# Decode block on one core: cache tiles loaded as K0 V0 K1 V1 K2 K3 V2 V3, the output weights as one load, and up's first sums ahead of gate's turn

## The chip, the core and the metric

The kernel runs on one core of one Trainium2 chip. A core has five engines that each work through their own queue: TensorE (PE in the profile, with its weight loads as PEld), VectorE (DVE), ScalarE (ACT), GpSimd (POOL) and SyncE (SP), which here only issues DMAs. The DMAs run on 16 DMA engines. The metric is the device time of one execution in microseconds (us).

## What is computed

One token goes through a pre-norm transformer block: attention over a cache of 4096 positions with 32 heads of 128, and a gated feed-forward of width 1728. All tensors are bf16, the model width is 640.

```python
def block(x, k_cache, v_cache, wq, wo, w_gate, w_up, w_down):
    q = (layernorm(x) @ wq)                  # 32 heads of 128
    scores = q . k_cache * 128 ** -0.5       # 32 x 4096
    p = softmax(scores)
    o = p @ v_cache                          # 32 x 128
    h = x + o.reshape(4096) @ wo             # 640
    g, u = layernorm(h) @ w_gate, layernorm(h) @ w_up    # 1728
    return h + (gelu(g) * u) @ w_down        # 640
```

Each weight and each cache entry is used once. K and V caches are 33.6 MB each, wq and wo 5.2 MB each, the three feed-forward weights 2.2 MB each.

## The kernel before

**Tiles and slots.** The heads are taken in four groups G of eight. A tile is the K or the V of one group: 128 partitions (16 for each head) by 256 positions by 128, which is 64 KB in each partition. Three slots of that size in on-chip memory hold everything large: slot 2 first holds wq, slots 0 and 1 the first K and V; then the tiles follow each other through the slots in load order (`home`). At the end wo lies in slot 2 and the feed-forward weights in slot 0; slot 1 takes small rows of the tail.

**Order of work.** The program is written out by hand. `Prog` (line 39) keeps one list of operations for each engine with their dependences; `emit` turns these into semaphore waits. What stands in an engine's list runs in that order. All large loads are issued by SyncE (`dma`, line 60), in the order in which they stand in the program: an issue whose wait isn't over holds back all that follow it. A load waits until the tile that it overwrites has been read (`done`).

The load order before is wq, K0, V0, K1, V1, K2, V2, K3 (in two halves), V3, wo (two halves of 16 heads' rows), then w_down's last rows, w_gate, w_up in two parts, and the rest of w_down in six. K1 waits for the use of wq, V1 for K0, K2 for V0, V2 for K1, K3 for V1, V3 for K2, wo for V2 and the feed-forward weights for K3.

**Scores.** For each group there are eight chunks c of 32 positions. `score_mult` (L315) multiplies K by q in place on VectorE, 128 x 4096 elements; its `fold` (L323 and, through the helper `matmul_again`, L29) sums the products on TensorE by eight matmuls against the identity into one of two PSUM banks, c % 2; `score_sum` (L332) reduces that bank on VectorE. VectorE's list is multiply c, then the sum of c - 1, so that it works while TensorE folds.

**Softmax and values.** `softmax` (L337 to L346) makes the exponentials on ScalarE and spreads them on VectorE into `mix`, the left operand of `attend` (L358): 64 matmuls of 128 x 512 against V. The source calls a group of 16 of them `pv`. In the kernel before `attend(G)` stands right behind `softmax(G)` on TensorE, and so ahead of the folds of group G + 1. `pick(G)` (L364 to L368) takes each head's part out of the result on VectorE; it stands behind the first sum of the next group. `head_sum(G)` (L372, L374) adds up the partitions of each head on TensorE, at c = 3.

**Output projection.** Two groups of heads share a result of 16 rows. `normalize(t)` (L378, L379) divides by the softmax sums, `spread(t)` (L382) and `take(t)` (L386, L391) turn it into columns `aP`, and `proj_part(t)` (L403 and L29) multiplies these by half t of wo in 32 matmuls. The first half runs for t = 0 within group 2's chunks 4 to 6 and behind the last `attend`; t = 1 follows at the end.

**Feed-forward.** The projection's rows are turned into columns (L462 to L470), added to x, normalized (L276 to L282, L479). `glu` (L490) makes gate and up in 20 matmuls each; `turn` (L496, L500, L503) copies such a row and turns it into columns, by VectorE for gate and by ScalarE for up. `resid` (L510) puts h into the output's bank. TensorE's list is gate, `resid`, gate's turn, up's first 12 matmuls, its last 8, and up's turn. VectorE and ScalarE make the gelu (L518 to L525), `down` (L540) multiplies by w_down in 57 matmuls in the order of the parts' loads, and the row is copied (L557, L559) and written out.

Of the kernel before, what the change touches and what calls it, by code (L numbers as in the profile page):

```python
# [5 lines left out]
FP32 = mybir.dt.float32  # L6
BF16 = mybir.dt.bfloat16
# [103 lines left out]
def bass_sequential_preLN__gqa_block_cached__glu_gated_geglu__decode_kernel(nc, A_x, A_k_cache, A_v_cache, A_wq, A_wo, B_x, B_w_gate, B_w_up, B_w_down, out):  # L111
# [17 lines left out]
    rz = sb("rz", [16, 2], FP32)  # L129
    po_r = sb("po_r", [128, 2, DH + 1], FP32)  # L130
    m4 = sb("m4", [128, 4], FP32)
    hs = sb("hs", [128, 24], FP32)
    hb = sb("hb", [128, 24], FP32)
    hbx = sb("hbx", [128, 8, 4], BF16)
    aT = sb("aT", [16, 2, 128], BF16)
    aP = sb("aP", [128, 2, 16], BF16)
    sel = sb("sel", [16, 16, 8], BF16)
    m8 = sb("m8", [128, 8], FP32)
    aM = sb("aM", [128, 8, 16], FP32)
# [34 lines left out]
    m8_t = first_t.take(128).rearrange("p (a b) -> p a b", a=8)  # L174
# [21 lines left out]
    wo_sb = slots[2][:, 0:32 * D].rearrange("p (t i n) -> p t i n", t=2, i=16)  # L196
# [18 lines left out]
    def load(kind, G, half, *deps):  # L215
        src = A_k_cache if kind == "K" else A_v_cache
        src = src[0, 8 * G:8 * G + 8, :, :].rearrange("h (p r) d -> (h p) (r d)", p=16)
        lo, hi = (0, SLOT) if half is None else (SLOT // 2 * half, SLOT // 2 * half + SLOT // 2)
        landed[(kind, G, half)] = P.dma("sync", home[(kind, G)][:, lo:hi], src[:, lo:hi], *deps)
# [5 lines left out]
    load("K", 0, None)  # L225
    load("V", 0, None)
# [18 lines left out]
    c_hb = mask(hb[:, 8:16], ones_b[:, 0:8], [[-16, 8]], 0, 1, ALU.is_ge, c_bz)  # L245
    c_hb = mask(hb[:, 8:16], hb[:, 8:16], [[16, 8]], 15, -1, ALU.is_ge, c_hb)
# [7 lines left out]
    c_sel = mask(sel[:, :, :], ones_b[0:16, 0:128].rearrange("p (a b) -> p a b", a=16), [[1, 16], [0, 8]], 0, -1, ALU.is_equal)  # L254
    c_m8 = mask(m8_t, ones_b[:, 0:128].rearrange("p (a b) -> p a b", a=8), [[-1, 8], [-8, 16]], 0, 1, ALU.is_equal)
# [3 lines left out]
    c_odd = V(lambda e: e.reduce_sum(odd[:, :], hb[:, 8:16].rearrange("p (a b) -> p b a", b=2), axis=AX.X), c_hb)  # L259
    c_far = V(lambda e: e.tensor_scalar(far[:, :, :], odd[:, :].unsqueeze(2).to_broadcast([128, 2, 16]), -1e38, 1e38, ALU.mult, ALU.add), c_odd)  # L260
    c_m4 = V(lambda e: e.reduce_sum(m4[:, :], m4_t, axis=AX.X), c_m4)
    c_m8 = V(lambda e: e.reduce_sum(m8[:, :], m8_t, axis=AX.X), c_m8)
    c_hs = V(lambda e: e.reduce_sum(hs[:, 8:16], hs_t.rearrange("p a b c -> p a (b c)"), axis=AX.X), c_hs, c_hz)
# [38 lines left out]
    free2 = [qd, c_sel2, c_par, c_m4, c_m8, c_hs, c_idb]  # L302

    folds, reds, exps, pbs, pvs, mks, evs, hds, nbs = {}, {}, {}, {}, {}, {}, {}, {}, {}
    z4s, spr, aPs = {}, {}, {}
# [6 lines left out]
    def score_mult(G, c):  # L312
        kt = tile("K", G)[:, 32 * c:32 * c + 32, :]
        got = landed.get(("K", G, None)) or landed[("K", G, c // 4)]
        m = V(lambda e: e.tensor_tensor(out=kt, in0=kt, in1=qb[:, G, :].unsqueeze(1).to_broadcast([128, 32, DH]), op=ALU.mult),  # L315
              got, q1)
        again, held[0] = held[0], True

        def fold(e):
            for b in range(8):  # L320
                args = (ps_f[c % 2][:, :], id_b[:, :], kt[:, :, 16 * b:16 * b + 16])
                if b == 0 and not again:
                    i = e.matmul(*args, start=True, stop=False)  # L323
                else:
                    i = matmul_again(nc, *args, b == 0, b == 7, (128, 128), (0, 0))
            return i
        folds[(G, c)] = T(fold, m, c_idb, reds.get((G, c - 2) if c >= 2 else (G - 1, c + 6)))
        if c == 7:
            done[("K", G)] = folds[(G, c)]
# [22 lines left out]
    def attend(G):  # L352
        vt = tile("V", G)
        for n in range(PARTS):
            def pv(e, n=n):
                for c in range(64 // PARTS * n, 64 // PARTS * (n + 1)):
                    a = 32 * (c % 4)
                    i = e.matmul(po[a:a + 32, 0:512], p_bd[:, c, :], vt[:, 4 * c:4 * c + 4, :],  # L358
                                 start=(c < 4), stop=(c >= 60))
                return i  # L360
            pvs[G] = done[("V", G)] = other(pv, pbs[(G, n)], landed[("V", G, None)], mks.get(G - 1))
# [15 lines left out]
    def normalize(t):  # L377
        rc = V(lambda e: e.reciprocal(rz[:, t:t + 1], ps_a[0:16, 132 * t + DH:132 * t + DH + 1]), hds[2 * t + 1])  # L378
        z4s[t] = V(lambda e: e.tensor_scalar(aT[:, t, :], ps_a[0:16, 132 * t:132 * t + DH], rz[:, t:t + 1], None, ALU.mult), rc)  # L379

    def spread(t):
        spr[t] = other(lambda e: e.matmul(ps_z[:, 32:160], sel[:, :, :].rearrange("p a b -> p (a b)"), aT[:, t, :], start=True, stop=True),  # L382
                       z4s[t], c_sel)

    def take(t):
        m = V(lambda e: e.tensor_tensor(out=aM[:, :, :], in0=ps_z[:, 32:160].rearrange("p (q i) -> p q i", q=8),  # L386
                                        in1=m8[:, :].unsqueeze(2).to_broadcast([128, 8, 16]), op=ALU.mult), spr[t], c_m8)

        def fn(e):
            with nc.allow_low_precision(reason="one of the eight terms is not zero"):  # L390
                return e.reduce_sum(aP[:, t, :], aM[:, :, :].rearrange("p q i -> p i q"), axis=AX.X)  # L391
        aPs[t] = V(fn, m)

    def proj_part(t, lo, hi, *ws):
        def fn(e):
            for i4 in range(lo, hi, 4):
                for half in range(2):
                    for i in range(i4, i4 + 4):
                        a = 32 * (i - i4)
                        args = (bank[half][a:a + 1, 0:320], aP[:, t, i:i + 1], wo_sb[:, t, i, 320 * half:320 * half + 320])  # L400
                        start, stop = t == 0 and i < 4, t == 1 and i >= 12
                        if half == 0:
                            r = e.matmul(*args, start=start, stop=stop)  # L403
                        else:
                            r = matmul_again(nc, *args, start, stop, (128, 32), (0, a))
            return r
        return T(fn, *ws)

    PARTS = 4
    for G in range(NG):  # L410
        for c in range(8):
            score_mult(G, c)
            if c >= 1:
                score_sum(G, c - 1)
            if c == 1 and G:
                pick(G - 1)
            if c == 3 and G:
                head_sum(G - 1)
            if c == 4 and G == 2:
                normalize(0)  # L420
            if c == 5 and G == 2:
                spread(0)
            if c == 6 and G == 2:
                take(0)
        score_sum(G, 7)
        softmax(G)
        if G == 0:
            load("K", 1, None, *free2)
            load("V", 1, None, done[("K", 0)])
        attend(G)  # L430
        if G == 0:
            load("K", 2, None, done[("V", 0)])
        if G == 1:
            load("V", 2, None, done[("K", 1)])
            for h in range(2):
                load("K", 3, h, done[("V", 1)])
        if G == 2:
            load("V", 3, None, done[("K", 2)])
# [153 lines left out]
```

## Time and profile before

| | |
|---|---|
| time, median of 3 runs | 202.01 us (201.98 to 202.13) |
| the profiled execution's own time | 202.1 us |
| its span, first to last instruction | 200.9 us |
| bytes read | 84.23 MB, 419 GB/s over the span |
| busy: PE, PEld, DVE, ACT, POOL | 110.0, 17.7, 118.5, 6.8, 4.2 us |
| mean granted TensorE clock | 0.832 |

The profile shows one execution. Its page gives each engine's busy time, the span in 40 slices (a digit is the busy share in tenths, PEclk the granted clock), the DMA queues, the chain of work that ended last, the costliest groups of instructions and the DMA issues with the time from issue to landing. The trace behind it answers by timeline: start, duration, engine, line, operation, tiles and, in brackets, how long the engine had been idle and what released it. By stretches it gives each engine's busy time, then three figures: granted clock, mean share of the DMA engines in use, GB/s. SPq stands for SyncE's queue, where the issues are.

The chain that ended last is 51% DMA, 30% DVE and 16% PE. The longest group is the multiply of L315, 32 times 2282 ns.

### The profile page before, as it was taken

Reading aid. Unit: us, or ns where it says so; the run is one execution under the profiler, and the core shown is the slowest. Engines: PE = TensorE matmul, PEld = TensorE weight load, DVE = VectorE, ACT = ScalarE, POOL = GpSimd, SP = SyncE. Lnnn points to the kernel's source line nnn. Section 1 sums busy time; section 2 is a strip of 40 time slices with the busy share of each in tenths; the row PEclk is TensorE's granted clock in tenths of the full one; section 3 lists DMA queues with packets and bytes.
Section 4 is the critical chain, followed back from the end, with each engine's and each line's share of the span. In section 5 each row is a group of like instructions: output and inputs, shape, how many; then the busy total and the mean of one; then the engine's idle time right before and its main releaser. Section 6 shows DMA issues by size and latency. Waiting matters only on the chain.

```text
span 200.9 us, 1518 instructions
## 1 busy us (share of the span) xinstructions
PE 110.0 (55%) x771; PEld 17.7 (9%) x491; DVE 118.5 (59%) x160; ACT 6.8 (3%) x18; POOL 4.2 (2%) x19
## 2 busy tenths in 40 slices
PE   0108000686665708776745196856394777394584
PEld 0103000000002200000011000000120000131322
DVE  3300100889975027999750569897869997624331
ACT  2100000000001000000010000000100000100111
POOL 7100000000000000000000000000000000000000
PEclk9999855599996665899979757999789999888567
DMA  9999999999999999999999999799999998999993
GB/s 359 416 478 418 418 418 418 418 431 483 522 431 418 396 431 431 418 431 418 418 418 434 444 522 431 339 418 424 431 502 421 431 431 372 445 404 441 404 408 108
DMA packets 3178, 84.32 MB, mean 420 GB/s; under 512 B 354, under 2 KB 868, under 8 KB 1380
## 3 DMA queue, kind: packets, MB, share of 16 engines
q1 hardware_dynamic: 3170, 84.23, 97.8%
q8 instruction: 5, 0.08, 0.2%
q14 instruction: 1, 0.01, 0.0%
q10 hardware_dynamic: 2, 0.00, 0.0%
HBM read 84.23 MB, written 0.00 MB: 419 GB/s over the span
## 4 chain that ended last, share of the span: by engine, by line
DMA 51%; DVE 30%; PE 16%; SPq 1%; issue 1%; ACT 0%
DMA slot<-in_A_k_cache_dram 39%; DVE slot L315 21%; DMA slot<-in_B_w_down_dram 12%; PE bank L29 8%; DVE sc L332 6%; PE bank L358 6%; SPq L60 1%; PE bank L323 1%; DVE mix L364 1%; PE bank L540 1%; DVE mix L346 0%; DVE mix L367 0%; DVE mx L337 0%; ACT p_t L342 0%; DVE po_r L368 0%
## 5 line engine op out<-in xcount | busy, mean ns | idle before, releaser
L315 DVE TENSOR_TENSOR slot<-slot,qb 128x4096 bf16<-128x4096 bf16 x32 | 72.7, 2282 | 32.7 <-DMA slot<-in_A_k_cache_dram 32.7
L29 PE MATMUL bank<-slot,id_b 128*128 128x512 bf16 x248 | 66.2, 419 | 21.7 <-DVE slot L315 21.7
L332 DVE TENSOR_REDUCE sc<-bank 128x32 f32<-128x512 f32 x32 | 21.9, 685 | 12.4 <-PE bank L29 12.4
L358 PE MATMUL bank<-slot,mix 128*32 128x512 bf16 x256 | 22.1, 521 | 12.3 <-DVE mix L346 12.3
L323 PE MATMUL bank<-slot,id_b 128*128 128x512 bf16 x8 | 3.8, 471 | 33.5 <-DVE slot L315 33.5
L358 PEld LDWEIGHTS bank<-slot,mix 128*32 128x32 bf16 x256 | 8.3, 126 | 72.1 <-DVE mix L346 61.3
L297 PE MATMUL bank<-slot,xlnM 128*32 128x512 bf16 x40 | 4.5, 630 | 7.3 <-DMA slot<-in_A_wq_dram 7.3
L342 ACT ACTIVATE p_t<-sc,nb 128x256 bf16<-128x256 f32 x4 | 2.0, 507 | 161.8 <-DVE nb L341 161.8
L346 DVE TENSOR_TENSOR mix<-p_t,hbx 128x512 bf16<-128x512 bf16 x16 | 5.7, 420 | 2.7 <-ACT p_t L342 2.7
L301 DVE CAST qb<-bank 128x512 bf16<-128x512 f32 x1 | 0.7, 692 | 10.3 <-PE bank L297 10.3
L490 PE MATMUL bank<-slot,hlnT 128*1 128x512 bf16 (+1 forms) x40 | 4.6, 551 | 1.5 <-DVE hlnT L479 1.5
L364 DVE TENSOR_TENSOR mix<-bank,m 128x512 f32<-128x512 f32 x4 | 2.7, 684 | 4.4 <-PE bank L358 4.4
L270 PE MATMUL bank<-one_bf,slot 1*128 1x1 bf16 x5 | 0.4, 177 | 6.8 <-DMA slot<-in_A_x_dram 6.8
L323 PEld LDWEIGHTS bank<-slot,id_b 128*128 128x128 bf16 x8 | 0.8, 98 | 36.8 <-DVE slot L315 36.3
L372 PEld LDWEIGHTS bank<-po_r,hb 128*16 128x16 f32 x8 | 0.5, 94 | 36.6 <-issue 36.5
L403 PE MATMUL bank<-slot,aP 128*1 128x320 bf16 x32 | 2.2, 299 | 1.0 <-DMA slot<-in_A_wo_dram 1.0
L540 PE MATMUL bank<-slot,hm 128*1 128x128 bf16 (+2 forms) x57 | 2.2, 255 | 0.7 <-DMA slot<-in_B_w_down_dram 0.7
L297 PEld LDWEIGHTS bank<-slot,xlnM 128*32 128x32 bf16 x40 | 1.6, 140 | 9.4 <-issue 9.4
L29 PE MATMUL bank<-slot,aP 128*1 128x320 bf16 x32 | 2.2, 299 | 0.0
L557 DVE CAST slot<-bank 1x128 bf16<-1x128 f32 (+1 forms) x2 | 0.6, 316 | 2.4 <-PE bank L540 2.4
L374 PE MATMUL bank<-po_r,hs 128*16 128x128 f32 x8 | 1.5, 272 | 0.5 <-DVE po_r L368 0.5
L367 DVE TENSOR_TENSOR mix<-mix 128x256 f32<-128x256 f32 x4 | 1.7, 424 | 0.1
(91 smaller groups left out, 40.7 us busy)
## 6 DMA issues: line engine op xcount, KB each, us to landing
slot<-in_A_k_cache_dram SPq DMA_DIRECT2D x2, 4096.0 KB, 38.0
slot<-in_A_wq_dram SPq DMA_DIRECT2D x1, 5120.0 KB, 15.4
slot<-in_A_wo_dram SPq DMA_DIRECT2D x2, 2560.0 KB, 30.9
slot<-in_B_w_gate_dram SPq DMA_DIRECT2D x1, 2160.0 KB, 17.1
slot<-in_B_w_up_dram SPq DMA_DIRECT2D x1, 1296.0 KB, 19.7
slot<-in_B_w_down_dram SPq DMA_DIRECT2D x2, 640.0 KB, 23.0
slot<-in_B_w_up_dram SPq DMA_DIRECT2D x1, 864.0 KB, 21.4
slot<-in_B_w_down_dram SPq DMA_DIRECT2D x1, 480.0 KB, 24.3
```

The lines of the kernel that those rows point to most:

```text
L29: return e.add_instruction(mybir.InstMatmult(name=nc.get_next_instruction_name(), engine=e.engine, start_tensor_calc=start, stop_tensor_ca ...
L60: ev = self.op(eng, lambda e: e.dma_start(out, in_), *deps, dma=True)
L297: i = e.matmul(ps_q[32 * j:32 * j + 32, :], xlnM[:, 160 * s + 32 * c:160 * s + 32 * c + 32], wq_j[:, c, 2 * j + s, :, :], start=(c == 0 an ...
L315: m = V(lambda e: e.tensor_tensor(out=kt, in0=kt, in1=qb[:, G, :].unsqueeze(1).to_broadcast([128, 32, DH]), op=ALU.mult), got, q1)
L323: i = e.matmul(*args, start=True, stop=False)
L332: reds[(G, c)] = V(lambda e: e.reduce_sum(sc[:, 32 * c:32 * c + 32], ps_f[c % 2][:, :].rearrange("p (g d) -> p g d", d=16), axis=AX.X), fo ...
L346: pbs[(G, n)] = pbs[G] = V(lambda e, lo=lo, hi=hi: e.tensor_tensor(out=p_bd[:, lo:hi, :].rearrange("p c (a r) -> p c a r", a=8), in0=p_t[: ...
L358: i = e.matmul(po[a:a + 32, 0:512], p_bd[:, c, :], vt[:, 4 * c:4 * c + 4, :], start=(c < 4), stop=(c >= 60))
L364: mks[G] = V(lambda e: e.tensor_tensor(out=po_m, in0=po[:, 0:512].rearrange("p (b d) -> p b d", b=4), in1=m4[:, :].unsqueeze(2).to_broadca ...
L403: r = e.matmul(*args, start=start, stop=stop)
L490: i = e.matmul(po[32 * a:32 * a + 1, 512 * k:512 * k + n], hlnT[:, c:c + 1], w[:, c, 512 * a:512 * a + n], start=(c == 0), stop=(c == 4))
L540: i = e.matmul(ps_d[32 * q:32 * q + 1, a - lo:b - lo], w, wd_sb[:, m, a - base:b - base], start=False, stop=(m == 12), skip_group_check=(m ...
```

## The change

Six things are edited.

- The load order becomes K0 V0 K1 V1 K2 K3 V2 V3, every tile in one load. K3 now waits for K1, V2 for V1, V3 for K2. K3 lies in slot 2 and V2 in slot 0.
- wo becomes one load. It waits for K3, whose slot it takes; the feed-forward weights, which stand behind it in SyncE's list, wait for V2.
- `attend(2)` moves from behind `softmax(2)` to chunk 5 of group 3, between the folds of chunks 4 and 5. `pick(2)` moves to chunk 7 of group 3 and `head_sum(2)` behind `softmax(3)`.
- The four groups share one result of 32 rows. `head_sum` puts each group's sums into it by masks of 32 columns. `normalize` runs once, at the end, with the spreading and taking in it.
- `proj` runs once, 64 matmuls behind the landing of all of wo.
- TensorE's list in the tail becomes gate, up's first 12 matmuls, gate's turn, up's last 8, `resid`, up's turn.

Masks grow or go with it: `hs` and `hb` have 56 columns instead of 24, `sel` is 32 x 32 x 4, and the mask `m8` is no longer made.

```diff
-    order = [(kind, G) for G in range(NG) for kind in "KV"]
+    order = [("K", 0), ("V", 0), ("K", 1), ("V", 1), ("K", 2), ("K", 3), ("V", 2), ("V", 3)]
     for n, t in enumerate(order):
         home[t] = slots[n % 3][:, :]
-    home[("K", 3)], home[("V", 2)] = slots[0][:, :], slots[2][:, :]
...
     def head_sum(G):
-        g, at = G % 2, 132 * (G // 2)
-        other(lambda e: e.matmul(ps_a[0:16, at + DH:at + DH + 1], hb[:, 8 - 8 * g:24 - 8 * g], po_r[:, g, DH:DH + 1],
-                                 start=(g == 0), stop=(g == 1), skip_group_check=True), exps[G], z4s.get(G // 2 - 1), c_hb)
-        hds[G] = T(lambda e: e.matmul(ps_a[0:16, at:at + DH], hs[:, 8 - 8 * g:24 - 8 * g], po_r[:, g, 0:DH],
-                                      start=False, stop=(g == 1), skip_group_check=True), evs[G], c_hs)
+        lo = 24 - 8 * G
+        other(lambda e: e.matmul(ps_a[0:32, DH:DH + 1], hb[:, lo:lo + 32], po_r[:, G % 2, DH:DH + 1],
+                                 start=(G == 0), stop=(G == 3), skip_group_check=True), exps[G], c_hb)
+        hds[G] = T(lambda e: e.matmul(ps_a[0:32, 0:DH], hs[:, lo:lo + 32], po_r[:, G % 2, 0:DH],
+                                      start=False, stop=(G == 3), skip_group_check=True), evs[G], c_hs)
...
         for c in range(8):
+            if c == 5 and G == 3:
+                attend(2)
             score_mult(G, c)
             if c >= 1:
                 score_sum(G, c - 1)
-            if c == 1 and G:
+            if c == 1 and G in (1, 2):
                 pick(G - 1)
-            if c == 3 and G:
+            if c == 3 and G in (1, 2):
                 head_sum(G - 1)
-            if c == 4 and G == 2:
-                normalize(0)
-            if c == 5 and G == 2:
-                spread(0)
-            if c == 6 and G == 2:
-                take(0)
+            if c == 7 and G == 3:
+                pick(2)
         score_sum(G, 7)
         softmax(G)
...
-        attend(G)
+        if G == 3:
+            head_sum(2)
+        if G != 2:
+            attend(G)
...
         if G == 1:
-            load("V", 2, None, done[("K", 1)])
-            for h in range(2):
-                load("K", 3, h, done[("V", 1)])
+            load("K", 3, done[("K", 1)])
+            load("V", 2, done[("V", 1)])
...
-    d_wo = [P.dma("sync", wo_sb[:, t, :, :], A_wo[2048 * t:2048 * t + 2048, :].rearrange("(p i) n -> p i n", i=16), done[("V", 2)])
-            for t in range(2)]
-    free = done[("K", 3)]
+    d_wo = P.dma("sync", slots[2][:, 0:32 * D], A_wo[:, :].rearrange("(p i) n -> p (i n)", i=32), done[("K", 3)])
+    free = done[("V", 2)]
...
     pick(NG - 1)
-    proj_part(0, 0, 16, aPs[0], d_wo[0], reds[(NG - 1, 7)])
     head_sum(NG - 1)
-    normalize(1)
-    spread(1)
-    take(1)
-    pr = proj_part(1, 0, 16, aPs[1], d_wo[1])
+    aPd = normalize()
+    pr = T(proj, aPd, d_wo, reds[(NG - 1, 7)])
...
     ga = T(glu(0, wg_sb, range(5)), hl, d_wg, mks[NG - 1])
+    T(glu(1, wu_sb, range(3)), d_wu[0], c_po)
+    ga = turn(0, ps_g, ga, z0)
+    up = T(glu(1, wu_sb, range(3, 5)), d_wu[1])
     T(resid, hx, c_onef)
-    ga = turn(0, ps_g, ga, z0)
-    T(glu(1, wu_sb, range(3)), d_wu[0], c_po)
-    up = T(glu(1, wu_sb, range(3, 5)), d_wu[1])
```

More of the change, by code (lines that the diff above doesn't have):

```diff
@@ L207, in bass_sequential_preLN__gqa_block_cached__glu_gated_geglu__decode_kernel, with load @@
     home = {}
-    order = [(kind, G) for G in range(NG) for kind in "KV"]
+    order = [("K", 0), ("V", 0), ("K", 1), ("V", 1), ("K", 2), ("K", 3), ("V", 2), ("V", 3)]
     for n, t in enumerate(order):
         home[t] = slots[n % 3][:, :]
-    home[("K", 3)], home[("V", 2)] = slots[0][:, :], slots[2][:, :]
     tile = lambda kind, G: home[(kind, G)].rearrange("p (k d) -> p k d", d=DH)
     landed, done = {}, {}
-    def load(kind, G, half, *deps):
+    def load(kind, G, *deps):
         src = A_k_cache if kind == "K" else A_v_cache
         src = src[0, 8 * G:8 * G + 8, :, :].rearrange("h (p r) d -> (h p) (r d)", p=16)
-        lo, hi = (0, SLOT) if half is None else (SLOT // 2 * half, SLOT // 2 * half + SLOT // 2)
-        landed[(kind, G, half)] = P.dma("sync", home[(kind, G)][:, lo:hi], src[:, lo:hi], *deps)
+        landed[(kind, G)] = P.dma("sync", home[(kind, G)], src, *deps)
     A(lambda e: e.preload_act_table_set("natural_log_exp_and_others"))
@@ L224, in bass_sequential_preLN__gqa_block_cached__glu_gated_geglu__decode_kernel @@
     d_wq = P.dma("sync", wq_sb, A_wq[:, :].rearrange("(p c) n -> p (c n)", c=5))
-    load("K", 0, None)
-    load("V", 0, None)
+    load("K", 0)
+    load("V", 0)
     c_one = V(lambda e: e.memset(one_bf[:, :], 1.0))
@@ L313, in score_mult @@
         kt = tile("K", G)[:, 32 * c:32 * c + 32, :]
-        got = landed.get(("K", G, None)) or landed[("K", G, c // 4)]
         m = V(lambda e: e.tensor_tensor(out=kt, in0=kt, in1=qb[:, G, :].unsqueeze(1).to_broadcast([128, 32, DH]), op=ALU.mult),
-              got, q1)
+              landed[("K", G)], q1)
         again, held[0] = held[0], True
@@ L360, in pv @@
                 return i
-            pvs[G] = done[("V", G)] = other(pv, pbs[(G, n)], landed[("V", G, None)], mks.get(G - 1))
+            pvs[G] = done[("V", G)] = other(pv, pbs[(G, n)], landed[("V", G)], mks.get(G - 1))
     def pick(G):
@@ L377, in normalize @@
[L377 to L387, printed above, removed]
-        def fn(e):
-            with nc.allow_low_precision(reason="one of the eight terms is not zero"):
-                return e.reduce_sum(aP[:, t, :], aM[:, :, :].rearrange("p q i -> p i q"), axis=AX.X)
-        aPs[t] = V(fn, m)
@@ L394, in proj_part @@
[L394 to L407, printed above, removed]
+        lo = 24 - 8 * G
@@ new lines, in head_sum, with normalize @@
+        other(lambda e: e.matmul(ps_a[0:32, DH:DH + 1], hb[:, lo:lo + 32], po_r[:, G % 2, DH:DH + 1],
+                                 start=(G == 0), stop=(G == 3), skip_group_check=True), exps[G], c_hb)
+        hds[G] = T(lambda e: e.matmul(ps_a[0:32, 0:DH], hs[:, lo:lo + 32], po_r[:, G % 2, 0:DH],
+                                      start=False, stop=(G == 3), skip_group_check=True), evs[G], c_hs)
+    def normalize():
+        rc = V(lambda e: e.reciprocal(rz[:, :], ps_a[0:32, DH:DH + 1]), hds[3])
+        z = V(lambda e: e.tensor_scalar(aT[:, :], ps_a[0:32, 0:DH], rz[:, 0:1], None, ALU.mult), rc)
+        sp = T(lambda e: e.matmul(ps_z[:, 32:160], sel[:, :, :].rearrange("p a b -> p (a b)"), aT[:, :], start=True, stop=True), z, c_sel)
+        m = V(lambda e: e.tensor_tensor(out=aM[:, :, :], in0=ps_z[:, 32:160].rearrange("p (q i) -> p q i", q=4),
+                                        in1=m4[:, :].unsqueeze(2).to_broadcast([128, 4, 32]), op=ALU.mult), sp, c_m4)
+        def fn(e):
+            with nc.allow_low_precision(reason="one of the four terms is not zero"):
+                return e.reduce_sum(aP[:, :], aM[:, :, :].rearrange("p q i -> p i q"), axis=AX.X)
+        return V(fn, m)
@@ new lines, in proj @@
+    def proj(e):
+        for i4 in range(0, 32, 4):
+            for half in range(2):
+                for i in range(i4, i4 + 4):
+                    a = 32 * (i - i4)
+                    args = (bank[half][a:a + 1, 0:320], aP[:, i:i + 1], wo_sb[:, i, 320 * half:320 * half + 320])
+                    if half == 0:
+                        r = e.matmul(*args, start=(i < 4), stop=(i >= 28))
+                    else:
+                        r = matmul_again(nc, *args, i < 4, i >= 28, (128, 32), (0, a))
+        return r
```

41 lines of the change are left out of this document (18 added, 23 removed).

## The prediction

> **What bounds the kernel now.** I read the page's slices and DMA queues first, then the chain that ended last, then the timeline of the attention loop and the tail.
>
> ```profile
> DMA  9999999999999999999999999799999998999993
> q1 hardware_dynamic: 3170, 84.23, 97.8%
> slot<-in_A_wq_dram SPq DMA_DIRECT2D x1, 5120.0 KB, 15.4
> ```
>
> The 16 DMA engines are busy in all slices but the last: one stream of 84 MB in issue order, each load waiting its turn. Any time in which they have nothing issued is added to the end, and so is the tail behind the last landing. The last load (96 KB of w_down, issued 180.12, landing 18.7 us later by the DMA issues) is there at 198.8; the span ends at 200.9. So I ask of each moved load: is it issued before the one ahead of it runs out? These are SyncE's issues and the rows that the change moves against them:
>
> ```profile
> 34.76 4.50 DVE L315 TENSOR_TENSOR slot<-slot,qb 128x4096 bf16<-128x4096 bf16 x2 [14.03 <-DMA slot<-in_A_k_cache_dram]
> ...
> 59.60 0.33 SPq L60 DMA_DIRECT2D slot<-in_A_v_cache_dram  x1
> ...
> 140.58 0.33 SPq L60 DMA_DIRECT2D slot<-in_A_v_cache_dram  x1
> ...
> 144.51 4.49 DVE L315 TENSOR_TENSOR slot<-slot,qb 128x4096 bf16<-128x4096 bf16 x2
> ...
> 148.94 0.80 SPq L60 DMA_DIRECT2D slot<-in_A_wo_dram  x2
> ...
> 169.09 1.89 PE L29 MATMUL bank<-slot,id_b 128*128 128x512 bf16 x8 [0.91 <-DVE slot L315]
> 171.00 0.33 SPq L60 DMA_DIRECT2D slot<-in_B_w_down_dram  x1
> ...
> 183.26 0.31 PE L403 MATMUL bank<-slot,aP 128*1 128x320 bf16 x4 [1.05 <-DMA slot<-in_A_wo_dram]
> ...
> 188.94 1.87 PE L490 MATMUL bank<-slot,hlnT 128*1 128x512 bf16 x17 [1.49 <-DVE hlnT L479]
> ...
> 198.07 1.17 PE L540 MATMUL bank<-slot,hm 128*1 128x128 bf16 x20 [0.67 <-DMA slot<-in_B_w_down_dram]
> ```
>
> V3 is issued at 140.58 and lands on the last engine 30.3 us later, at 170.9; the trace's completion counts show the first engine done at 169.0. Behind it stands wo, issued at 148.94, 20 us early. The other weights wait for K3's last fold and go out at 171.00, covered by wo's 12 us on the engines. The profiled execution took 202.1 us, 1.2 over its span and 0.1 over the median of 202.01. The sum is made against it.
>
> **The change part by part.**
>
> *wo behind K3's last fold (the costly step).* wo's slot now holds K3, not V2, so wo waits for that fold, and the ten weight loads stand behind it on SyncE's queue although their own wait (PV of V2) is long over. When is the fold? K2 still lands fourth after wq, at 112.5. VectorE leaves K2's loop earlier by the first normalization: 129.69 to 130.14 (L378, L379) and 135.74 to 136.33 (L386, L391), 1.05 us. The first K3 multiply, at 144.51 before, comes at 143.5. K3's loop then has no PV ahead of its first fold and no pick at c=1, which makes it K0's loop: 34.76 to the issue released by its last fold at 59.60, 24.84 us, with a first fold at half clock (PE has been idle for 6 us in both). That gives 168.3.
>
> Now PV of V2 sits between folds 4 and 5. Its 64 matmuls took 5.25 us in group 2, 31 of them at half clock; the 33 after 146.95 took 1.9, so all at full clock take 3.7. Fold 5 then ends 1.93 + 3.7 + 1.9 = 7.55 us after multiply 4, where VectorE, with two sums (0.60) and two multiplies (2.20), has been ready since 5.6. The stall is 1.95 us. The pick at c=7 (1.4) lies beside fold 7. wo is issued at **170.3**, when the first engines have been dry for 1.3 us and the last is about to be.
>
> *Restart.* No run here shows a restart in mid-kernel, but the launch is one: wq, of wo's size and row length, was issued at 0.0; 15 engines finished it by 14.6 and the last at 15.4, where the packets alone (8 of 1.514 us on each engine) take 12.1. Nearest from below is the output, 1.1 us from issue to landing, which would give 13.2. I take 14.6, the same load from idle engines: wo lands at 184.9 (183.5 to 185.7), not at 183.1. The page "DMA: Bandwidth & Descriptors" of the Trainium skill (Specifications) puts the first byte of a SyncE load at about 0.6 us, where wq's first packet starts at 1.0; by the page the landing would be an estimated 184.5 and the time 204.2. Its rule to issue early and wait late (Rules for kernel authors) speaks against this edit, by the 20 us of lead above.
>
> *What follows wo on the engines.* From wo's landing to the last w_down landing is 15.7 us now (183.1 to 198.8), and the same bytes follow. The end of the stream is 184.9 + 15.7 = 200.6, later by **1.8**. By the trace's packets, wo's rows as one (1.514 for 40 KB) against two (2 x 0.766) save 0.02 x 8, and K3 whole 0.1, the latter lost in the gap.
>
> *All heads after wo.* Half of the projection is done at 179.2 now; afterwards all 64 matmuls wait for wo. The other input is earlier: attention of V3 starts about 0.7 sooner than its 174.06, so aP is there near 182.5, not on the path. Eight groups of four take 0.136 each at full clock; sixteen take 2.35. But what clock?
>
> ```profile
> 179.40:183.20 3.80, 1.70 (x37) 0.62 (x17) 2.56 (x7) 0.00 (x0) 0.00 (x0) 1.00 1.02 428
> 183.20:184.50 1.30, 1.24 (x32) 0.40 (x16) 0.00 (x0) 0.00 (x0) 0.00 (x0) 1.00 0.99 425
> 184.50:188.90 4.40, 1.31 (x16) 1.05 (x12) 2.39 (x11) 1.01 (x3) 0.00 (x0) 0.50 0.97 407
> ```
>
> In this view by stretches the third figure from the end is the granted clock. It fell to 0.50 at 184.5, behind 3.4 us in which PE was busy for 1.75. After the change PE is nearly idle for 6 us between the end of PV (178.8) and wo. So I take half clock: by 0.43 us for a group of four 512-wide matmuls, a 320-wide one takes 0.27, and sixteen with their end 4.4. The projection ends at 189.3, not 184.5. The clock-gate rule (Trainium skill, "TensorE: Matmul & The Clock Gate", Part 1: an idle window of 3.4 us halves the clock, a busy one restores it) agrees with this row.
>
> *Tail.* From the projection to the gate sums stays 4.42 us (184.52 to 188.94): gate starts at 193.7, when its weights have landed. There the reordering helps: up's first twelve matmuls cover VectorE's copy of the gate sums (0.69), and no DMA wait (0.79 now) is left. At half clock 40 matmuls are 4.3 (0.43 per four), the turn 0.5, then as now 1.47 from up's end to down, 0.1, and down's 57 matmuls without waits at 0.029 each, 1.65: the last ends 8.0 after gate's start, at 201.7. Now it ends at 199.24. The residual matmuls, moved behind up, run beside ScalarE's copy of up (0.59). So **+2.5** on the path through compute, above the +1.8 of the stream: the later of the two counts.
>
> *At nothing.* The larger masks and the mask less run on POOL and VectorE in the first 8 us, while q waits for wq until 15.4 (cover 7 us). Head sums with 32 columns instead of 16 stand in PE's idle time; those of group 2 run while PE waits 3 us for softmax of K3. K3 whole instead of in halves: it lands near 132, 12 us before its first multiply. K3 and V2 are still issued near 100 and 108, V3 near 139.5, each ahead of the load before it running out at about 111, 130 and 150.
>
> Sum: 202.1 + 2.5 = 204.6, or 204.5 beside the median.
>
> **Rivals.**
> - *The stream alone decides.* If PE is at full clock for the projection, it ends 2 us earlier, compute ends at 199.7, before the last landing, and the time is the stream's: 202.1 + 1.8 = 203.9; with a restart at its lower bound the two paths give 203.2 at half clock and, with full clock, 202.5. For it: the clock was 1.00 in the stretch before 183.2. Against: half of that stretch's work is the early projection that goes.
> - *A later fold.* K2's loop in this profile lost 0.7 to a second half-clock stretch (126.29, VectorE waiting for a fold). If that also hits K3, or PV in mid-loop, which costs up to 1.6 more at half clock, the issue is at 171 to 172: 205.3 to 206.2.
> - *The gap never opens (faster).* If K3's last fold is over by 167.5, wo is issued before the first engine is dry at 169.0 less the 1.0 us from wq's issue to its first packet. wo then lands at 183.1, compute (even with 2.35 for the projection) ends at 198.0, and the stream ends 0.2 earlier than now: 201.9. This needs PV to cost VectorE nothing and 0.8 more. Against: PE is idle for only 0.91 per chunk in this loop, so 3.7 us cannot hide behind one spare bank.
> - *The reordering doesn't do what it says*: now up waits for its weights at 193.7 anyway, so up ahead of gate's turn would be hidden; that is the previous case's tail and changes nothing there.
>
> **How the numbers follow.** Forecast (204.0 to 205.2) 0.45; stream alone or a quick restart (202.5 to 204.0) 0.23; later fold (205.2 to 206.3) 0.22; no gap 0.06; beyond 0.04. The range takes in the first three but for the low end of the second: 203.0 to 206.2. A measurement of this kernel can tell 0.2% (0.4 us) from no change. Faster has half of the no-gap case with a little of the unforeseen, 0.04, same 0.05, slower 0.91.
>
> **What would show it.** A DMA slice near 172 with a share well under 0.9 and wo's issue near 170.3, released by K3's last fold; an idle stretch of VectorE near 2 us ahead of its sum of chunk 5; wo 14 to 15 us from issue to landing; all projection matmuls behind it at clock 0.5; gate's start near 193.7. Wrong if wo is issued before 168, if the engines restart within 1 us, or if the projection runs at full clock.

## The result and the profile after

The changed kernel takes 204.69 us (median of five, 204.25 to 205.12) against 202.01: 1.0126 times as long, 95% interval 1.0115 to 1.0137. The prediction was 204.5 in a range of 203.0 to 206.2. The profiled execution took 204.25 with a span of 203.0. Medians and ratios here and below leave out slow runs, over 1.5% above the fastest of their kernel: two of the six with the wait alone (207.19 and 207.35) and one of the seven with the quarters (206.19). A ratio is estimated over all runs that count, so it need not be the quotient of the medians.

The page after: the DMA slices, how the chain that ended last is made up, and wo among the DMA issues (size, us from issue to landing).

```profile
DMA  9999999999999999999999999999999994999993
...
DMA slot<-in_A_k_cache_dram 39%; DVE slot L307 21%; PE bank L29 10%; DMA slot<-in_A_wo_dram 7%; DVE sc L324 6%; PE bank L350 4%; PE bank L470 2%; PE bank L388 1%; DVE mix L338 1%; PE bank L315 1%; PE bank L520 1%; DVE slot L444 0%; DVE mx L329 0%; ACT p_t L334 0%; DVE slot L537 0%
...
slot<-in_A_wo_dram SPq DMA_DIRECT2D x1, 5120.0 KB, 14.7
```

Slice 33, from 167.5 to 172.6, has a 4 where all others but the last have a 9: here the engines ran dry. wo stands on the chain with 7%, where the last w_down load had 12% before, and its 14.7 us from issue to landing are close to the 15.2 that this page has for wq, which is as large and met idle engines at the launch. The timeline after (line numbers of the changed kernel: L307 multiply, L324 sum, L350 PV, L388 and L29 projection, L470 gate and up, L520 down):

```profile
142.99 4.49 DVE L307 TENSOR_TENSOR slot<-slot,qb 128x4096 bf16<-128x4096 bf16 x2
...
159.29 3.64 PE L350 MATMUL bank<-slot,mix 128*32 128x512 bf16 x64
...
164.80 0.69 DVE L324 TENSOR_REDUCE sc<-bank 128x32 f32<-128x512 f32 x1 [1.78 <-PE bank L29]
...
167.74 1.89 PE L29 MATMUL bank<-slot,id_b 128*128 128x512 bf16 x8 [1.25 <-DVE slot L307]
...
169.66 0.33 SPq L60 DMA_DIRECT2D slot<-in_A_wo_dram  x1
...
184.46 0.43 PE L388 MATMUL bank<-slot,aP 128*1 128x320 bf16 x4 [5.27 <-DMA slot<-in_A_wo_dram]
...
188.41 0.31 PE L29 MATMUL bank<-slot,aP 128*1 128x320 bf16 x4
...
192.95 3.58 PE L470 MATMUL bank<-slot,hlnT 128*1 128x512 bf16 x32 [1.50 <-DVE hlnT L459]
...
199.53 1.83 PE L520 MATMUL bank<-slot,hm 128*1 128x128 bf16 x57
```

PV of V2 stands as a block of 3.64 us, and VectorE's sum of chunk 5 waits 1.78 us for the fold behind it. K3's last fold releases wo at 169.66. By the trace's completion counts 11 engines had finished V3 by 169.3 and the last did at 170.86; wo is there on all of them at 184.33. The same execution by stretches (busy time of each engine, then granted clock, DMA share, GB/s):

```profile
176.40:184.40 8.00, 0.63 (x3) 0.23 (x3) 2.56 (x7) 0.00 (x0) 0.00 (x0) 0.82 0.92 391
184.40:188.80 4.40, 4.26 (x64) 1.08 (x32) 0.02 (x1) 0.03 (x1) 0.00 (x0) 0.54 0.99 421
188.80:192.90 4.10, 1.09 (x12) 0.85 (x12) 2.36 (x11) 0.99 (x3) 0.00 (x0) 0.87 0.98 413
```

PE does 0.63 us of work in the 8 us ahead of wo, then the 64 matmuls in 4.26 us at a clock of 0.54. The trace has the clock at 0.5 from 181.6 to 188.4. The Trainium skill's rule of the idle window ("TensorE: Matmul & The Clock Gate", Part 1: about 3.4 us of it halve the clock) agrees with these rows.

### The profile page after: what moved, and what is told of

It reads as the page before. It is cut to its first block, busy times and chain, and to the rows that moved or that the text cites. A ratio compares the mean times of both kernels' runs of the same rounds, so it can differ in the third digit from the quotient of the medians.

```text
span 203.0 us, 1507 instructions
## 1 busy us (share of the span) xinstructions
PE 106.9 (53%) x770; PEld 17.0 (8%) x488; DVE 117.4 (58%) x155; ACT 6.6 (3%) x18; POOL 4.1 (2%) x18
## 4 chain that ended last, share of the span: by engine, by line
DMA 46%; DVE 31%; PE 20%; issue 1%; ACT 1%; SPq 0%; DVEq 0%
DMA slot<-in_A_k_cache_dram 39%; DVE slot L307 21%; PE bank L29 10%; DMA slot<-in_A_wo_dram 7%; DVE sc L324 6%; PE bank L350 4%; PE bank L470 2%; PE bank L388 1%; DVE mix L338 1%; PE bank L315 1%; PE bank L520 1%; DVE slot L444 0%; DVE mx L329 0%; ACT p_t L334 0%; DVE slot L537 0%
## 5 line engine op out<-in xcount | busy, mean ns | idle before, releaser
L307 DVE TENSOR_TENSOR slot<-slot,qb 128x4096 bf16<-128x4096 bf16 x32 | 72.7, 2283 | 33.3 <-DMA slot<-in_A_k_cache_dram 33.3
L29 PE MATMUL bank<-slot,id_b 128*128 128x512 bf16 x250 | 66.8, 419 | 26.6 <-DVE slot L307 26.6
L324 DVE TENSOR_REDUCE sc<-bank 128x32 f32<-128x512 f32 x32 | 22.0, 686 | 11.7 <-PE bank L29 11.7
L350 PE MATMUL bank<-slot,mix 128*32 128x512 bf16 x256 | 17.7, 440 | 8.7 <-DVE mix L338 8.7
L350 PEld LDWEIGHTS bank<-slot,mix 128*32 128x32 bf16 x256 | 7.3, 110 | 80.4 <-DVE mix L338 42.1
L388 PE MATMUL bank<-slot,aP 128*1 128x320 bf16 x32 | 3.8, 462 | 5.3 <-DMA slot<-in_A_wo_dram 5.3
L442 DVE CAST slot<-bank 97x320 bf16<-97x320 f32 x1 | 0.5, 492 | 8.9 <-PE bank L29 8.9
L470 PE MATMUL bank<-slot,hlnT 128*1 128x512 bf16 (+1 forms) x40 | 4.6, 552 | 1.5 <-DVE hlnT L459 1.5
L29 PE MATMUL bank<-slot,aP 128*1 128x320 bf16 x32 | 3.7, 451 | 0.0
L364 PEld LDWEIGHTS bank<-po_r,hb 128*32 128x32 f32 x8 | 0.6, 108 | 31.6 <-issue 31.4
L366 PE MATMUL bank<-po_r,hs 128*32 128x128 f32 x8 | 1.6, 280 | 1.6 <-DVE po_r L360 1.6
L520 PE MATMUL bank<-slot,hm 128*1 128x128 bf16 (+2 forms) x57 | 1.8, 230 | 0.0
## 6 DMA issues: line engine op xcount, KB each, us to landing
slot<-in_A_wq_dram SPq DMA_DIRECT2D x1, 5120.0 KB, 15.2
slot<-in_A_wo_dram SPq DMA_DIRECT2D x1, 5120.0 KB, 14.7
```

The source lines that it names most:

```text
L29: return e.add_instruction(mybir.InstMatmult(name=nc.get_next_instruction_name(), engine=e.engine, start_tensor_calc=start, stop_tensor_ca ...
L324: reds[(G, c)] = V(lambda e: e.reduce_sum(sc[:, 32 * c:32 * c + 32], ps_f[c % 2][:, :].rearrange("p (g d) -> p g d", d=16), axis=AX.X), fo ...
L388: r = e.matmul(*args, start=(i < 4), stop=(i >= 28))
L470: i = e.matmul(po[32 * a:32 * a + 1, 512 * k:512 * k + n], hlnT[:, c:c + 1], w[:, c, 512 * a:512 * a + n], start=(c == 0), stop=(c == 4))
L520: i = e.matmul(ps_d[32 * q:32 * q + 1, a - lo:b - lo], w, wd_sb[:, m, a - base:b - base], start=False, stop=(m == 12), skip_group_check=(m ...
```

## The experiments

A load's lead is the time from its issue to the moment at which the engines would run dry without it. The theory: wo's issue, late by its new wait, lets the engines run dry, and the whole projection behind wo, at half clock, keeps compute just behind the stream. Rivals: the gap alone; the projection alone; PV's new place or the tail. Ratios are against the kernel before on the same chip; the kernel before had medians of 202.16 and 202.17 there. "Profile" is each run's one profiled execution.

| run | median us | ratio, 95% interval |
|---|---|---|
| changed kernel | 204.69 | 1.0126, 1.0115 to 1.0137 |
| before + wo waits for K3 | 205.65 | 1.0154, 1.0112 to 1.0196 |
| changed, projection in halves | 205.62 | 1.0165, 1.0136 to 1.0195 |
| changed, order put back, K3 whole | 206.44 | 1.0216, 1.0177 to 1.0255 |
| changed, order put back, K3 in halves | 202.44 | 1.0018, 1.0003 to 1.0033 |
| before + new tail | 202.12 | 0.9996, 0.9984 to 1.0007 |
| changed, PV in quarters | 203.33 | 1.0052, 1.0034 to 1.0070 |
| changed, filling matmuls | 204.25 | 1.0113, 1.0086 to 1.0139 |
| changed, quarters and filling | 203.47 | 1.0063, 1.0043 to 1.0082 |
| changed, wo in two loads | 204.73 | 1.0126, 1.0103 to 1.0148 |
| changed, up's part ahead of wo | 205.99 | 1.0173, 1.0155 to 1.0191 |
| the same, with filling matmuls | 203.89 | 1.0089, 1.0066 to 1.0112 |
| order put back, K3 in halves, filling | 203.47 | 1.0044, 1.0021 to 1.0067 |

**The wait alone, on the kernel before.**

```diff
     d_wo = [P.dma("sync", wo_sb[:, t, :, :], A_wo[2048 * t:2048 * t + 2048, :].rearrange(...),
-                  done[("V", 2)])
+                  done[("K", 3)])
```

> The kernel before with one edit: the two loads of wo wait for K3's last fold instead of V2's PV; order of the work, projection and tail stay. Theory (the issue of wo comes after the engines have run dry): issue near 171.0 instead of 148.9, a dip in the DMA share there, second half of wo landing 14.7 us later at 185.7, the last w_down 15.7 to 16 us behind that, near 201.5; 204.5 to 205.0 us. Rival (the loss of the changed kernel is the whole projection behind wo and PV in mid-loop, not the issue): 202.0 to 202.4.

Measured: 205.65, with single times from 203.88 to 206.32. The rival falls: one wait, with nothing else changed, costs as much as the whole change (1.0154 against 1.0126, with intervals that overlap). The median lies 0.65 over the theory's range. In the profile, at 203.88 the lowest of all, K2's loop and PV had met a better clock (full from 120.6 to 171.8, where the kernel before has it at half from 123.1 to 126.5 and from 143.5 to 147.0), and the issue came early:

```profile
168.70 0.80 SPq L60 DMA_DIRECT2D slot<-in_A_wo_dram  x2
```

The last w_down then landed 31.9 us behind that issue, at 200.64, where I had counted 30.4 to 30.7. With an issue at 171.0, as K3's last fold had it in the profile of before, the same distance makes 206.2, near the slowest of these runs. The spread is wider too: of 17 runs of the kernel before on this chip, 16 lie between 201.99 and 202.33 and one at 203.36. There the loads that wait for K3's last fold have wo's 12 us on the engines ahead of them; here nothing is ahead of them, so a clock step in K2's or K3's loop can go straight into the time. With one profile for each kernel this link is argued, not shown.

**Everything but the order.** The load order, the waits and the places of group 2's PV, pick and head sum go back; one load of wo, one projection, the new tail stay.

```diff
-            if c == 5 and G == 3:
-                attend(2)
...
-            load("K", 3, done[("K", 1)])
-            load("V", 2, done[("V", 1)])
+            load("V", 2, done[("K", 1)])
+            load("K", 3, done[("V", 1)])
...
-    d_wo = P.dma("sync", ..., done[("K", 3)])
-    free = done[("V", 2)]
+    d_wo = P.dma("sync", ..., done[("V", 2)])
+    free = done[("K", 3)]
```

> The changed kernel with the load order, the places of PV, pick and head sum of group 2, and the waits of wo and the feed-forward weights as in the kernel before; one load of wo, one result of 32 rows, one projection of 64 matmuls and the tail's new order stay. Theory: wo is issued near 149, no gap, it lands at 183.1, the 64 matmuls run at half clock (4.3 us), the gate starts near 191.8 and the last matmul ends near 200.0: 202.7 to 203.1; at full clock 202.0. Rival (the gap is the whole loss): 202.0. Rival (order and gap are not the loss): 204.7.

Measured: 206.44. All three expectations missed, and the first line of K3's loop says why:

```profile
151.57 2.29 DVE L308 TENSOR_TENSOR slot<-slot,qb 128x4096 bf16<-128x4096 bf16 x1 [7.61 <-DMA slot<-in_A_k_cache_dram]
```

I had left K3 in one load. In the old order it comes behind V2, and all of it is there only at 151.5; VectorE needs the first half at 144. The halves of the kernel before were worth 7.6 us of VectorE's time, which the new order makes needless. So the run was made again with K3 in halves:

```diff
+        if (kind, G) == ("K", 3):
+            for h in range(2):
+                lo = SLOT // 2 * h
+                landed[(kind, G, h)] = P.dma("sync", home[(kind, G)][:, lo:lo + SLOT // 2], src[:, lo:lo + SLOT // 2], *deps)
+            return
```

> As the run with the order put back (one load of wo, one projection of 64 matmuls, the tail's new order; load order, waits and places of group 2's PV as in the kernel before), but with K3 loaded in halves as in the kernel before. There K3 as one load landed at 151.5, 7.6 us after VectorE was free for it, which hid what the run was made for. Theory: wo lands at 183.1, no gap, the 64 matmuls run at half clock until 187.5, gate starts near 191.8, the last matmul ends near 200.0: 202.7 to 203.1. At full clock: 202.0. Rival (the gap is the whole loss, a projection behind wo costs nothing): 202.0 with the projection seen at half clock.

Measured: 202.44. Of the 1.26% only 0.18% are left. Yet this profile (203.26, slower than ten of the other eleven runs) shows the projection just as late and slow as I had expected:

```profile
182.95 0.44 PE L394 MATMUL bank<-slot,aP 128*1 128x320 bf16 x4 [3.99 <-DMA slot<-in_A_wo_dram]
```

and the stretch from its start to its end (busy time of PE, PEld, DVE, ACT, POOL, then granted clock, DMA share, GB/s) shows a clock of 0.50:

```profile
182.90:187.40 4.50, 4.44 (x64) 1.07 (x32) 0.00 (x0) 0.00 (x0) 0.00 (x0) 0.50 1.00 424
```

Its last matmul ends at 200.27, 1.7 behind the last landing of 198.6. So in this run the whole projection at half clock makes compute the later path, and its 1.1 us over the kernel before (203.26 against 202.16) are the top of what I expected. The median is only 0.3 over. No trace shows whether the projection of the other runs met half clock; their range, 201.94 to 203.83, takes in the theory's times for full clock (202.0) and for half. Either way the order, with its waits and PV's place, is nearly all of the loss; the run with the wait alone has shown that wait by itself.

**The tail alone, on the kernel before.**

```diff
-    T(resid, hx, c_onef)
+    T(glu(1, wu_sb, range(3)), d_wu[0], c_po)
     ga = turn(0, ps_g, ga, z0)
-    T(glu(1, wu_sb, range(3)), d_wu[0], c_po)
     up = T(glu(1, wu_sb, range(3, 5)), d_wu[1])
+    T(resid, hx, c_onef)
```

> The kernel before with the tail's new order alone (up's first twelve matmuls ahead of gate's turn, the residual matmuls behind up). Theory: up waits for its weights until 193.7 and down for w_down until 198.8, so nothing changes: 201.8 to 202.2. Rival (the order of the tail is worth its 0.7 us of PE's wait for the copy): 201.3.

Measured: 202.12, 0.9996. The reordering is hidden behind the loads, as the prediction's last rival had it. Within the changed kernel, where the prediction counted on it, it was not tried by itself.

**PV in quarters.** Sixteen matmuls each between the folds of chunks 3 to 7.

```diff
-            if c == 5 and G == 3:
-                attend(2)
+            if c >= 4 and G == 3:
+                attend(2, [c - 4])
```

> The changed kernel with PV of group 2 in four quarters of 16 matmuls, one each between the folds of chunks 3 to 7 of K3, instead of all 64 between folds 4 and 5. Theory: a quarter (0.9 us) fits into PE's idle time per chunk (0.91), VectorE's stall of 1.8 us goes, wo is issued near 167.8 and lands near 183.1, the stream ends near 199.5; the projection still runs at half clock and decides: 203.2 to 203.6. Rival (PV's place is not what sets the issue): 204.7. Rival (the gap is the whole loss): 202.2.

Measured: 203.33, as the theory had it, but not all in the way it had it. PV's place thus carries, by way of wo's issue, about half of the loss (1.0126 falls to 1.0052). The stall is gone:

```profile
166.53 0.69 DVE L324 TENSOR_REDUCE sc<-bank 128x32 f32<-128x512 f32 x1
...
168.64 0.33 SPq L60 DMA_DIRECT2D slot<-in_A_wo_dram  x1
```

The sums wait for no fold now. In this profile K2's loop lost 0.8 to a second half-clock stretch, so the issue was at 168.6 and not 167.8. wo landed on the first engine at 182.7, but on the last at 184.67, 1.4 behind all others: by the packets, one engine started its first wo packet at 171.4, 2.8 us after the issue. The trace doesn't name the engines, so why that one came late stays open.

**Keeping the clock up.** Between the spreading and the projection TensorE gets 30 matmuls whose result is not used.

```diff
+    def warm(e):
+        for _ in range(30):
+            i = e.matmul(ps_q[:, 160:512], id_b[:, :], qb[:, :, :].rearrange("p g d -> p (g d)")[:, 0:352], start=True, stop=True)
+        return i
+    T(warm, q1)
     pr = T(proj, aPd, d_wo, reds[(NG - 1, 7)])
```

> The changed kernel with 30 matmuls more (128 x 352, their result unused) on TensorE between the spreading and the projection, where it is idle for 5.3 us waiting for wo. Theory: the clock stays 1.0, the projection takes 2.4 us instead of 4.3, but the stream that restarted 2 us late ends as before, near 201: 203.9 to 204.5, only 0.2 to 0.8 less than the changed kernel. Rival (the half clock is the loss): 202.6 or less. Rival (the clock doesn't matter at all): 204.7.

Measured: 204.25, within the theory's numbers, but the interval holds the changed kernel's ratio too, so no gain is shown. The timeline, with the filling (L443), the projection behind it and the last matmuls of `down` (L525):

```profile
181.62 4.65 PE L443 MATMUL bank<-qb,id_b 128*128 128x352 bf16 x30
186.20 0.31 PE L388 MATMUL bank<-slot,aP 128*1 128x320 bf16 x4
...
201.15 1.15 PE L525 MATMUL bank<-slot,hm 128*1 128x128 bf16 x20 [0.69 <-DMA slot<-in_B_w_down_dram]
```

The projection did run at full clock (2.4 us), and then TensorE waits 0.69 us for w_down at the end: the late stream decides, as the theory had it. But wo was issued late in this execution, at 170.5, and the filling lasted 1.2 us beyond wo's landing (185.04). That spoils part of the test.

> Both edits on the changed kernel: group 2's PV in quarters and the 30 filling matmuls ahead of the projection. Theory (issue of wo behind dry engines, and the whole projection at half clock, are the two terms; neither alone is all): 202.0 to 202.4, no more than the kernel before. Rival (something else in the change costs): above 203.

Measured: 203.47, no better than the quarters alone, and 1.1 over what the theory had. The stream is why: the chain that ended last is made of w_down's loads; wo was issued at 168.1 and landed on the first engine at 182.2 (181.2 in the kernel before), on the last at 184.55. The lead was 0.7 us (the first engine finished V3 at 168.8), less than the 1.0 that I had put as the limit, the delay of the first packet. The projection ran at full clock here, and it gained nothing.

**Closing the gap with another load.** Up's second part (864 KB) goes out ahead of wo, near 163.

```diff
+    d_wu1 = P.dma("sync", wu_sb[:, 3:5, :], B_w_up[...], done[("V", 2)])
     d_wo = P.dma("sync", slots[2][:, 0:32 * D], ..., done[("K", 3)])
...
-    d_wu = [P.dma("sync", wu_sb[:, 0:3, :], wu_v[:, 0:3, :]),
-            P.dma("sync", wu_sb[:, 3:5, :], wu_v[:, 3:5, :])]
+    d_wu = [P.dma("sync", wu_sb[:, 0:3, :], wu_v[:, 0:3, :]), d_wu1]
```

> The changed kernel with up's second part (864 KB, 2.0 us of the stream) issued ahead of wo: it waits for V2's PV alone and goes out near 163, so that the engines have work until 171 to 173 when wo is issued near 170. Theory (two paths end together): the stream has no gap and ends near 198.9, 2 us earlier, but wo lands near 185.0, 0.6 later than in the changed kernel, the projection stays at half clock and compute decides: 204.4 to 205.0. Rival (the gap alone is the loss): 202.0 to 202.4.

> Up's second part ahead of wo and the 30 filling matmuls ahead of the projection, both on the changed kernel. Theory: gap and half clock are taken away together; wo lands near 185.0, the projection takes 2.4 us, gate starts near 191.7, the last matmul ends near 199.8: 202.4 to 202.9, while each edit alone gives 204.2 or more. Rival (the two terms add up singly): each edit alone would already have shown its part.

Measured: 205.99 and 203.89. Theory and rival both missed the first, and the second is 1.0 over its theory. The projection's first row in the timeline of each says how, first without filling (this profile, at 207.5, is the slowest of its seven runs):

```profile
187.17 0.43 PE L388 MATMUL bank<-slot,aP 128*1 128x320 bf16 x4 [8.07 <-DMA slot<-in_A_wo_dram]
```

and with the filling matmuls:

```profile
185.74 0.31 PE L388 MATMUL bank<-slot,aP 128*1 128x320 bf16 x4 [2.16 <-DMA slot<-in_A_wo_dram]
```

wo was expected at 185.0. It was there on 15 engines by 185.2 in the first profile, and on the last at 187.0; in the second at 184.9 and 185.6. Again one engine came late. The clock shows here: 64 matmuls from 187.17 to 191.60 without filling, from 185.74 to 188.08 with it. 2.1 us lie between the medians, as much as the projection gains; the profiles differ in wo's landing as well, so how much is the clock's is not settled. That it counts more here than in the gap (0.4) fits compute being the only late path once wo comes behind another load: without filling the last matmul ends at 204.49, 3.9 behind the last landing.

**Two controls.** The projection and normalization of the kernel before within the changed order, and wo in two loads with the projection left whole:

```diff
-    d_wo = P.dma("sync", slots[2][:, 0:32 * D], A_wo[:, :].rearrange("(p i) n -> p (i n)", i=32), done[("K", 3)])
+    d_wo = [P.dma("sync", slots[2][:, 16 * D * t:16 * D * t + 16 * D], wo_v[:, 16 * D * t:16 * D * t + 16 * D], done[("K", 3)])
+            for t in range(2)]
```

> The changed kernel with the projection of the kernel before: two loads of wo, two results of 16 rows, the first half of the heads multiplied as soon as the first half of wo is there. Load order, wait for K3, PV in mid-loop and the tail's order stay changed. Theory (gap sets the stream, the whole projection at half clock adds up to 0.8 on top): wo's second half lands near 184.4, 32 matmuls take at most 2.2, the gate starts near 191, and the time is that of the stream, 203.7 to 204.0. Rival (the projection behind wo is the loss): near 202.0. Rival (it costs nothing, the stream alone decides): 204.7, as the changed kernel.

> The changed kernel with wo in two loads of 2560 KB instead of one of 5120 KB, both waiting for K3; the projection still waits for both. Theory: behind dry engines the second load's landing comes 15.3 to 15.5 us after the first one's issue, as in the run with the projection in halves, against 14.7 for one load; everything behind it is 0.7 later: 205.3 to 205.6. Rival (that run was slow because of its projection in halves): 204.7, as the changed kernel.

Measured: 205.62 and 204.73. The first missed on the slow side; I put it to the two loads, and the second run refuted that. What the halves also bring back is the first normalization in K2's loop: two stops of VectorE, 0.45 and 0.58 us in its profile, ahead of K3's last fold and so ahead of wo's issue. But in that profile (204.87, below the median) wo's issue is only 0.3 later than in the changed kernel's, at 169.95, so this doesn't account for the 0.9 us over the changed kernel; it was not tried by itself, and the cause stays open. The rival falls all the same: with half of the projection done early, the chain that ended last is made of w_down's loads, and the time is no better.

**Order put back, with filling.** The filling matmuls on the run with K3 in halves.

> The run with the order put back and K3 in halves (no gap, one load of wo, one projection, new tail), with the 30 filling matmuls ahead of the projection. Theory: its 0.3 us over the kernel before are the projection at half clock; with the clock at 1.0 the stream decides again: 201.8 to 202.1, the best of all, perhaps 0.1 under the kernel before by wo's longer rows. Rival: 202.4 as without them.

Measured: 203.47, from 201.88 to 204.47. In the profile the filling ran from 180.4 to 185.0 while wo had landed at 182.9: thirty matmuls are too many where wo comes 1.4 us earlier. So this says nothing on the clock. No version was clearly faster than the kernel before.

## Why the prediction was right

- **wo's issue**: 170.3 predicted, 169.66 in the profile. The first K3 multiply came at 142.99 (143.5), the stall was 1.78 (1.95).
- **The restart**: wo landed 14.67 us after its issue (14.6, from wq at the launch). By the trace's packets, ten engines start 0.95 to 1.15 us after the issue, and their first packet takes 2.0 to 2.6 us instead of 1.5; the other six start 1.3 to 2.1 after it and take 1.5 to 1.9. The 0.6 us to the first byte of the Trainium skill ("DMA: Bandwidth & Descriptors", Specifications) is not what these records show. Its rule to issue early (the same page, Rules for kernel authors) is borne out by the run with the wait alone.
- **The projection at half clock**: 184.46 to 188.73, 4.3 us (4.4). That it costs time in the changed kernel is not shown: filling alone gained nothing clear of the interval, and filling on top of the quarters gained nothing. In the profiles with the projection at full clock behind the gap the stream decides.
- **The way to the gate** took 4.2 us (4.42), and from gate's start to the last matmul 8.4 (8.0), 0.26 of it a wait for w_down.
- **The stream behind wo** is the term that was mis-sized: 16.7 us from wo's landing to the last landing (184.33 to 201.06), not 15.7. From w_gate on one engine is 1.0 behind the others (190.66 against 189.67); the trace has a 16 KB instruction load (a piece of the program itself) at 188.2, 1.0 us long. The kernel before has one at 186.6, but there w_gate's last landing is 5.3 behind wo's, against 6.3 here; on which engine each fell the trace doesn't say. The +1.8 of the stream was +2.2, and the last matmul ended at 201.35, only 0.3 later. The two paths end together, which neither the forecast (compute) nor its first rival (stream) had said.
- **At nothing**: PV of V3 ran at full clock (3.64, not 5.3), so aP was there at 179.9 instead of 182.5, which changes nothing while wo lands at 184.3.
- **Luck in the number**: the profile is the fastest of the five runs, and in it compute ended 0.35 earlier than forecast (201.35, not 201.7) and the stream 0.5 later (201.06, not 200.6). What makes the median run 0.4 slower no trace shows, so part of the agreement of 204.5 with 204.69 is luck.
- **Rivals**: the later fold was not seen in a profile of the changed kernel; nearest is the run with filling, whose issue at 170.5 goes with 205.18. "The gap never opens" needed an issue by 167.5; no run with wo behind K3 had its profile's issue ahead of 168.1.

What stays open: the share of the half clock, since the filling matmuls twice outlasted the wait and, where they didn't, gained nothing behind the gap and at most 2.1 us with up's part ahead of wo; and which engine comes late and why.

## What to carry to other kernels

When loads follow each other through few slots, the price of a wait is set by what is behind it in the queue: ask of each load how long before the engines run dry it is issued. Here a lead of 0.7 us still cost time and one of 20 cost none; between them only 1.5 us was tried (wo behind up's part), and there wo landed 2.5 and 3.9 us later than in the kernel before, of which up's part itself makes about 2.0. A load that waits for the last step of a compute loop, with nothing queued ahead of it, puts that loop and every stall in it on the path. One load of a tile is as good as two only when nobody can start with the first half.

## What the runs showed of the hardware

- An issue that finds idle engines costs 1.5 to 2.2 us on each of them: in the profile of the changed kernel 3.05 to 3.7 us pass from wo's issue to the end of an engine's first packet, which takes 1.51 in full flow. Not all engines start together: one of the 16 began 2.0 to 2.8 us after the issue in the profiles of the changed kernel (171.8), with filling (172.5), with quarters (171.4) and with quarters and filling (170.8), where most of the rest started within 1.2. Engines that are still busy can go on without a break: in the last of these profiles, three whose V3 packets end at 170.16, 170.42 and 170.49, 2.1 to 2.4 us after the issue, start wo at just these times, with packets of 1.51. The trace doesn't name engines; they are told apart by packets that follow each other.
- Where the stream decides and no load comes late, times repeat closely: the kernel before with the new tail stays within 201.97 and 202.38, and 16 of 17 runs of the kernel before on that chip within 0.35. Where compute sets a load's issue or ends last, the same work spreads wider: 0.9 us in the changed kernel, 2.4 with the wait alone, and 1.9 with the order put back and K3 in halves, where no load comes late but, in the profile, compute ends 1.7 behind the stream.
- Whole rows don't matter by themselves: in the changed kernel, wo as one load with rows of 40 KB or as two with rows of 20 KB gives 1.0126 both times.
